# Elu of the first MoE handled in stages several products apart, with six tiles for the exponentials and another order of products

## The chip, the core and the metric

The program runs on one core of one Trainium2 chip. The metric is the device time of one execution in microseconds (us). Three timed runs of the kernel before gave 707.75, 708.32 and 710.72 us; the median is 708.32 us. The profiled execution took 708.1 us, 706.3 us of which are its span, from the first to the last instruction; 1.8 us lie around it.

## The reference

Attention with a pooled query gives `x` of 1152 tokens by 512; two feed-forward blocks follow. All is float32. The change concerns the first block:

```python
h = x @ w_in                                        # 1152x512 @ 512x2048
g = np.where(h > 0.0, h, alpha * (np.exp(np.minimum(h, 0.0)) - 1.0))   # Elu, alpha = 1
x = g @ w_out                                       # 1152x2048 @ 2048x512
```

The second block normalises `x` (root mean square), and computes `silu(xn @ w_gate) * (xn @ w_val) @ w_out`.

## The kernel before, in words

**Number format.** Every float32 operand is split in two parts, `h` (rounded) and `l` (the rest). A product with one 128-row slice is three matmuls, `h*h`, `l*h` and `h*l`, of 128 columns of weights against 384 tokens. Weights arrive as 64-bit words and are decoded on the chip. In the text a *matmul* is one of 128x384, a *product* is 12 of them (four slices, L216 to L218), a *half product* is 6, and a *group* (L712) is 6.

**Engines.** PE multiplies. ScalarE (ACT) does the Elu's Relu and Exp, the rounding to `h`, and two steps of each weight's decoding (L120, L122) and its rounding (L183). VectorE (DVE) does `max(exp - 1, v)`, called the *maximum* below (L237, L780), the sums of products, and three steps of the decoding (L131, L133, L136). GpSimd (POOL) computes the rest `l` (L64) and, for pairs of weights, the sums that the split product needs (L156 to L162). Each engine takes its instructions strictly in the order in which the program issues them: an instruction that waits holds up all behind it on its engine.

**The stream of weights.** `ws` is a generator of the decoding's steps. `ws.step(i, k)` issues the next k steps; the kernel calls it after every product, so that decoding is spread over the engines' queues. `ws.get(i)` issues steps until weight i is done. Weights are numbered w0 to w31 for the first block: per quarter q (four quarters of the 2048 hidden columns) four of `w_in` (8q to 8q+3), then four of `w_out` (8q+4 to 8q+7).

**The first block.** The tokens are three chunks c of 384, the hidden columns four quarters q of four slices i. `g(c, i)` is the Elu's output for a chunk and a slice.

- Quarter 0: twelve products, three of them (chunk 0, into the tile `fb`) at the end of attention, then nine in the order (i, c). Each is followed by `elu` (L230): Relu and Exp on ACT, the step before's rounding and rest (`flush`), the maximum on DVE.
- Quarters 1 to 3: for chunks 0 and 1 two slices at a time are computed as a 2x2 block product with seven multiplications (`Branch.m`, cases 1 to 7, one group each), chunk 2 with plain products (cases 8 and 9). Two branches, *even* and *odd*, make a quarter's *Elu stage* of 132 matmuls. Case 6 leaves a sum in the bank `b` that DVE reads for `u2` (L748), case 7 accumulates onto the same bank, after which DVE reads it for `u3` (L753), and case 4 accumulates once more. Results go through `Elu.out` (L769): the sum `v` (L774), Relu, Exp, then the maximum at the next `flush` and rounding and rest at the one after.
- After the stage come the quarter's *out products*: 12 products of `g` with `w_out` (`out1`, L841), for output slices m of 0 to 3 and chunks 2, 0, 1. Slice m=0 is done in halves: hidden slices 0 and 1 for all three chunks, then 2 and 3.
- `sums_from_x` (L798) makes the operands `ts` of the block product from `x`: four sums, four differences of 128x768 (L805, L809) on DVE, four roundings, four rests. It is stepped during quarter 0.
- In quarter 3 squares of `x` are added up for the root mean square (`Norm.square`, L668), and `Norm.sums` (L677) multiplies them by ones.

**Banks.** PSUM has eight banks. `bank()` (L645) hands out seven in turn; the eighth holds `wm` of the decoding, from the sixth bank on. A bank can be written again when its last reader is done.

Of the kernel before, what the change touches and what calls it, by code (L numbers as in the profile page):

```python
# [39 lines left out]
def tile_kernel(ctx: ExitStack, tc: tile.TileContext, qd, kd, vd, w1d, w2d, wgd, wvd, wod, rgd, outd):  # L40
# [207 lines left out]
    actx = ExitStack()  # L248
    ap = actx.enter_context(tc.tile_pool(name="attn", bufs=1))
    with tc.using_default_side("right"):  # L250
        sp = actx.enter_context(tc.tile_pool(name="psS", bufs=1, space=PSUM))
    pp = actx.enter_context(tc.tile_pool(name="psO", bufs=1, space=PSUM))
# [371 lines left out]
    early(2)  # L624
    for n in range(NE):
        elu(fb[:, n, 0:CH], ge[0][:, n, :], ge[1][:, n, :], lo_pool)
    actx.close()
# [8 lines left out]
    x2 = cp.tile([128, 4, NT], F32, name="x2")  # L636
    psb = [ctx.enter_context(tc.tile_pool(name="psB", bufs=5, space=PSUM))]
    nbank = 0

    def bank():  # L640

        nonlocal nbank
        n, nbank = nbank % 7, nbank + 1
        if n == 5 and len(psb) == 1:
            with tc.using_default_side("right"):  # L645
                psb.append(ctx.enter_context(tc.tile_pool(name="psC", bufs=2, space=PSUM)))
                ws.bank = ctx.enter_context(tc.tile_pool(name="psW", bufs=1, space=PSUM))
        return psb[n >= 5].tile([128, 512], F32, tag="b", name="b", bufs=2 if n >= 5 else 5)[:, 0:CH]
# [8 lines left out]
    th, tl = (tsp.tile([128, 12, CH], F32R, name=f"ts{a}", tag=f"ts{a}") for a in "hl")  # L657
    ts = [(xh[:, 0:2, cs(1)], xl[:, 0:2, cs(1)])] + [(th[:, 2 * n:2 * n + 2], tl[:, 2 * n:2 * n + 2]) for n in range(3)]
    sums_at = [[t.rearrange("p k c -> p (k c)")[:, a:a + 1024].rearrange("p (k c) -> p k c", k=8) for t in (th, tl)]
               for a in (2304, 3584)]  # L660

    class Norm:
# [40 lines left out]
    class Branch:  # L703
# [11 lines left out]
        def m(self, n):  # L715
# [10 lines left out]
            elif n == 2:  # L726
                self.group(self.a, a12, b21, False, True)
                flush()
                self.out(0, 0, self.a)
                self.both(n)  # L730
            elif n == 3:
                self.group(self.e, s(4), b22, False, True)
                flush()
                self.out(0, 1, self.e, self.u2)
            elif n == 4:
                self.group(self.b, a22, ts[3], False, True)
                flush()
                self.out(1, 0, self.b, self.m1)
            elif n == 5:
                self.e = bank()  # L740
                self.group(self.e, s(1), ts[0], True, False)
                flush()
            elif n == 6:
                self.b = bank()
                self.group(self.b, s(2), ts[1], True, False)
                flush()
                self.u2 = hp.tile([128, CH], F32, tag="e", name="u2", bufs=4)
                V.tensor_tensor(out=self.u2, in0=self.b, in1=self.m1, op=ALU.add)  # L748
            elif n == 7:
                self.group(self.b, s(3), ts[2], False, False)  # L750
                flush()
                self.u3 = self.pool.tile([128, CH], F32, tag="u3", name="u3", bufs=2)
                V.tensor_tensor(out=self.u3, in0=self.b, in1=self.m1, op=ALU.add)  # L753
                self.both(n)
            else:
                b = bank()
                product(b, w[n - 8], xchunk(2), True, True)
                flush()
                self.out(n - 8, 2, b)

    class Elu(Branch):
# [6 lines left out]

        def out(self, k, c, p, add=None):  # L769
            h, l = g_block(c, self.k + k)  # L770
# [5 lines left out]
            T.activation(out=e, in_=v, func=AF.Relu, scale=-1.0)  # L776
            T.activation(out=e, in_=e, func=AF.Exp, scale=-1.0)

            def second():
                V.scalar_tensor_tensor(out=e, in0=e, scalar=-1.0, in1=v, op0=ALU.add, op1=ALU.max)  # L780
                pending.append(third)

            def third():
                T.copy(h, e)  # L784
                lo_pool(l, e, h)

            pending.append(second)

        def both(self, n):
            if n == 7:  # L790
                self.out(1, 1, self.e, self.u3)
# [7 lines left out]
    def sums_from_x():  # L799

        r = x2.rearrange("p m c -> p (m c)")[:, NT:NT + 3072].rearrange("p (n k c) -> p n k c", n=4, k=2)
        b11, b12, b21, b22 = (r[:, n] for n in (0, 1, 2, 3))
        for n, (j, l) in enumerate(((0, 0), (0, 1), (1, 0), (1, 1))):
            h, l = (t[:, 2 * j:2 * j + 2, cs(l)] for t in (xh, xl))
            V.tensor_tensor(out=r[:, n], in0=f(h), in1=f(l), op=ALU.add)  # L805
            yield
        t1, t2, t3, t4 = b11, b22, b12, b21
        for n, o, a, b in ((0, t1, b12, b11), (2, t3, b22, b12), (1, t2, b22, t1), (3, t4, b21, t2)):
            V.tensor_tensor(out=o, in0=a, in1=b, op=ALU.subtract)  # L809
            yield  # L810
        for n, t in ((0, t1), (2, t3), (1, t2), (3, t4)):
            T.copy(ts[n][0], t)
            yield
            (lo_dve if n in (0, 3) else lo_pool)(ts[n][1], t, ts[n][0])
            yield

    sums_of_x = sums_from_x()

# [3 lines left out]
    for i in range(4):  # L822
        w = ws.get(i)
        for c in range(3):
            if c == 0 and i < NE:
                continue
            ps = bank()
            product(ps, w, xchunk(c), True, True)
            elu(ps, *g_block(c, i), lo_pool)
            if i > 1:  # L830
                next(sums_of_x)
        wi += 1

    for q in range(4):
        if q:
# [3 lines left out]
            run([(b, 1), (old, 4), (b, 8), (old, 3)], 2 * q + 2)  # L839
            run([(b, k) for k in (2, 9, 6, 5, 7, 4, 3)], 2 * q + 3)  # L840
            ws.limit = 2 * q + 4  # L841
            wi += 4

        def out1(c, m, b, then=None, ks=range(4)):
            product(b, ws.get(wi + m if q == 3 else wi), lambda k: g_block(c, k), True, True, ks)
            flush()
# [14 lines left out]
        if q < 3:  # L861
            for m in range(4):
                bs = [bank() for c in range(3)]
                for ks in ((0, 1), (2, 3)) if m == 0 else (range(4),):
                    for c in (2, 0, 1):
                        out1(c, m, bs[c], None, ks)
                        if q == m == 0:
                            next(sums_of_x, None)
                            next(sums_of_x, None)
                        ws.step(wi, 5 if len(ks) > 2 else 3)  # L870
                wi += 1
        else:
# [21 lines left out]
    class Gate(Branch):  # L894


        def __init__(self, n):
            super().__init__([ws.get(wi + 2 * n + k) for k in range(2)], up)
            self.sums, self.val, self.i = n + 6, n % 2, 2 * (n // 2)

        def out(self, k, c, p, add=None, into=None):
            d = u[c][:, self.i + k]
# [6 lines left out]
            else:  # L909
                pending.append(lambda: T.activation(out=d, in_=p, func=AF.Silu))  # L910

# [181 lines left out]
```

## Time and profile before

| | |
|---|---|
| median of three runs | 708.32 us (707.75 to 710.72) |
| profiled execution | 708.1 us, span 706.3 us |
| PE busy | 675.0 us, 96% |
| DVE, ACT, POOL busy | 509.3, 473.1, 451.4 us |
| attention and first products | 0 to 273 us |
| out products of quarter 0 | 273 to 306 us |
| quarters 1, 2, 3 | from 306 us to 482 us |
| second block | 482 to 706 us |

How to read it: the busy share of PE is an average. What a change is worth is read where PE stands idle: which instruction it waited for, how long, and at what clock it went on. The granted clock of a stretch is written as a share of full speed; it has two levels, 1.2 and 2.4 GHz, so 0.5 would be a stretch wholly at the lower one.

### The profile page before, as it was taken

The page shows a single profiled execution, that of the slowest core. Times are in us where ns is not written, and L with a number is a line of the kernel's source. Part 1 is how long each engine was busy: PE and PEld are TensorE (multiplying, and loading weights), DVE is VectorE, ACT ScalarE, POOL GpSimd, SP SyncE. Part 2 cuts the span into 40 slices and gives each one's busy share as a digit, 9 for nine tenths or more (in the row PEclk, how much of TensorE's full clock was granted, in tenths as well). Part 3 has the DMA queues.
Part 4 walks back from the last instruction along what each step waited for, and adds up shares of the span by engine and source line. Part 5 has one row for each costly group of instructions (what it writes and reads, how often), then busy time and mean ns, then how long its engine had stood idle before and what let it go on. Part 6 is the DMA issues. An engine that isn't in the chain of part 4 may idle for free. (4 is left out here: it accounts for less than half of the span.)

```text
span 706.3 us, 11416 instructions
## 1 busy us (share of the span) xinstructions
PE 675.0 (96%) x4149; PEld 663.4 (94%) x4149; DVE 509.3 (72%) x867; ACT 473.1 (67%) x924; POOL 451.4 (64%) x409
## 2 busy tenths in 40 slices
PE   8999999999999997997997898799999999999998
PEld 7999999999999996997996898799999999999997
DVE  7989989998998859855665664568778866867300
ACT  6888989888899868577547556654766655545400
POOL 5998889888895237676566474455898966233200
PEclk9999999999999999898999899899999999999999
DMA  5533332233221002230331132020234322303200
GB/s 167 178 110 127 101 115 84 93 131 130 98 86 47 1 31 90 90 120 30 105 106 60 60 112 67 31 90 31 70 111 141 104 85 90 120 1 120 97 34 33
DMA packets 21624, 61.75 MB, mean 87 GB/s; under 512 B 2752, under 2 KB 5056, under 8 KB 21568
## 3 DMA queue, kind: packets, MB, share of 16 engines
q1 hardware_dynamic: 21568, 61.03, 26.0%
q8 instruction: 32, 0.52, 0.3%
q14 instruction: 24, 0.20, 0.1%
HBM read 58.66 MB, written 2.36 MB: 86 GB/s over the span
## 5 line engine op out<-in xcount | busy, mean ns | idle before, releaser
L64 POOL TENSOR_TENSOR wl<-wt,wh 128x512 fp32r<-128x512 f32 x68 | 92.2, 1355 | 79.5 <-ACT wh L183 77.9
L70 DVE TENSOR_TENSOR ptl<-t,pth 128x384 fp32r<-128x384 f32 x216 | 106.7, 549 | 5.2 <-ACT pth L364 4.7
L342 DVE TENSOR_SCALAR_CACHE_REDUCE p<-s 128x1152 f32<-128x1152 f32 x72 | 97.3, 1353 | 14.7 <-PE s L338 14.0
L364 ACT CAST pth<-t 128x384 fp32r<-128x384 f32 x216 | 89.2, 488 | 21.6 <-PE t L356 20.8
L338 PE MATMUL s<-kd,qt 128*128 128x384 f32 x480 | 98.6, 342 | 1.8 <-DVE p L342 1.0
L347 ACT ACTIVATE p<-p,st 128x1152 f32<-128x1152 f32 x72 | 91.5, 1271 | 1.3 <-DVE p L342 1.1
L216 PE MATMUL b<-xh,wh 128*128 128x384 f32 x260 | 88.2, 339 | 0.0
L217 PE MATMUL b<-xl,wh 128*128 128x384 f32 x260 | 88.2, 339 | 0.0
L218 PE MATMUL b<-xh,wl 128*128 128x384 f32 x260 | 88.2, 339 | 0.0
L338 PEld LDWEIGHTS s<-kd,qt 128*128 128x128 f32 x480 | 81.2, 189 | 5.2 <-DVE p L342 2.7
L382 PE MATMUL o<-pth,vd 128*128 128x256 f32 (+1 forms) x288 | 84.4, 315 | 0.0
L356 PE MATMUL t<-ident,p 128*128 128x128 f32 x648 | 82.5, 273 | 0.0
L382 PE MATMUL o<-ptl,vd 128*128 128x256 f32 (+1 forms) x288 | 78.5, 295 | 0.0
L356 PEld LDWEIGHTS t<-ident,p 128*128 128x128 f32 x648 | 75.0, 141 | 2.0 <-ACT p L347 0.3
L120 ACT ACTIVATE we<-wr 128x512 uint32<-128x512 uint32 x68 | 45.5, 669 | 39.4 <-DMA wr<-in_w_dram 18.7
L122 ACT ACTIVATE wm<-wr 128x512 f32<-128x512 f32 x62 | 38.9, 628 | 30.4 <-DVE wt L136 30.2
L131 DVE TENSOR_SCALAR wm<-wm 128x512 f32<-128x512 f32 x62 | 43.0, 693 | 18.8 <-ACT wm L122 18.7
L216 PE MATMUL b<-gh,wh 128*128 128x384 f32 x144 | 50.3, 349 | 4.7 <-ACT gh L238 4.7
L382 PEld LDWEIGHTS o<-pth,vd 128*128 128x128 f32 x288 | 54.4, 189 | 0.3
L382 PEld LDWEIGHTS o<-ptl,vd 128*128 128x128 f32 x288 | 54.5, 189 | 0.0
L64 POOL TENSOR_TENSOR gl<-eg,gh 128x384 fp32r<-128x384 f32 x27 | 27.4, 1016 | 42.3 <-ACT gh L784 42.3
L217 PE MATMUL b<-gl,wh 128*128 128x384 f32 x144 | 50.1, 348 | 2.8 <-POOL gl L64 2.8
(200 smaller groups left out, 1808.3 us busy)
## 6 DMA issues: line engine op xcount, KB each, us to landing
wr<-in_w_dram SPq DMA_DIRECT2D x32, 512.0 KB, 3.2
rawq<-in_q_dram SPq DMA_DIRECT2D x15, 576.0 KB, 4.2
rawk<-in_k_dram SPq DMA_DIRECT2D x28, 288.0 KB, 2.9
wr<-in_wg_dram SPq DMA_DIRECT2D x12, 512.0 KB, 3.2
wr<-in_wv_dram SPq DMA_DIRECT2D x12, 512.0 KB, 3.2
wr<-in_wo_dram SPq DMA_DIRECT2D x12, 512.0 KB, 3.3
rawv<-in_v_dram SPq DMA_DIRECT2D x16, 288.0 KB, 2.8
out_dram<-o SPq DMA_DIRECT2D x12, 192.0 KB, 1.8
```

Of the source, the lines that this page charges most:

```text
L64: G.tensor_tensor(out=o, in0=i, in1=f(h), op=ALU.subtract)
L70: V.tensor_tensor(out=o, in0=i, in1=f(h), op=ALU.subtract)
L120: T.activation(out=e, in_=lo, func=AF.Copy, scale=0.93625 * 2.0 ** -29)
L216: PE.matmul(out, lhsT=wh[:, k, :], rhs=ah, start=first and k == 0, stop=False)
L217: PE.matmul(out, lhsT=wh[:, k, :], rhs=al, start=False, stop=False)
L218: PE.matmul(out, lhsT=wl[:, k, :], rhs=ah, start=False, stop=last and k == 3)
L338: PE.matmul(s[:, m, 0:384], lhsT=a, rhs=b[:, 384 * m:384 * m + 384], start=n == 0, stop=n == len(parts) - 1)
L342: V.tensor_scalar(out=pt, in0=s[:, :, 0:384], scalar1=-0.0625, scalar2=None, op0=ALU.mult, op1=ALU.min, accum_out=st[p][:, 0, TILES[i][4], :])
L347: T.activation(out=pt, in_=pt, func=AF.Exp, scale=-1.0, bias=st[p][:, 0, TILES[i][4], :], accum_out=st[p][:, 1, TILES[i][4], :])
L356: PE.transpose(ps[:, k, :], src[:, 128 * b:128 * b + 128], ident)
L364: T.copy(oh, re(ps))
L382: PE.matmul(self.o[:, 0:self.N], lhsT=v[:, b, :], rhs=(pth, ptl)[u][:, g["buf"], b, g["c0"]:320], start=self.n == 0, stop=self.n == 17)
```

## The change

In short: (1) `elu` and `Elu.out` become one function; each result's maximum is issued two calls of `flush` later, its rounding and rest three later, and `flush` is called within `elu`, after the sum. (2) The tiles `e` for the exponentials are six in place of three, in the block's own pool. (3) The sum `v` is written back into the product's bank (or into `u3`) in place of an own tile `v`. (4) In case 6, `u2` is issued ahead of `flush`. (5) The odd branch runs cases 6, 5, 2, 7, 9, 4, 3 in place of 2, 9, 6, 5, 7, 4, 3. (6) In quarters 0 to 2 the out products of m=0 and m=1 are both done in halves, so that six half products lie between the Elu stage and the first use of hidden slices 2 and 3; the weight of m=1 is needed three half products earlier. (7) `sums_from_x` issues its four sums before the first Elu, the differences one every three products, the rest between the out products. (8) The banks are four and three in place of five and two, and `wm` has its bank earlier. (9) The last addition of squares moves from POOL to DVE.

```diff
+    def defer(n, work):
+        pending.append([n, work])
     def flush():
-        now, pending[:] = list(pending), []
-        for work in now:
+        for item in pending:
+            item[0] -= 1
+        due = [work for n, work in pending if n == 0]
+        pending[:] = [item for item in pending if item[0]]
+        for work in due:
             work()
-    def elu(ps, gh, gl, lo):
-        e = hp.tile([128, CH], F32, tag="e", name="e", bufs=4)
-        T.activation(out=e, in_=ps, func=AF.Relu, scale=-1.0)
+    def elu(v, gh, gl, add=None, into=None):
+        e = gp.tile([128, CH], F32, tag="eg", name="eg", bufs=6)
+        if add is not None:
+            ps, v = v, v if into is None else into
+            V.tensor_tensor(out=v, in0=ps, in1=add, op=ALU.add)
+        flush()
+        T.activation(out=e, in_=v, func=AF.Relu, scale=-1.0)
         T.activation(out=e, in_=e, func=AF.Exp, scale=-1.0)
-        flush()
-        ws.step(wi, 1)
-        V.scalar_tensor_tensor(out=e, in0=e, scalar=-1.0, in1=ps, op0=ALU.add, op1=ALU.max)
-        pending.append(lambda: (T.copy(gh, e), lo(gl, e, gh)))
-        ws.step(wi, 2)
+        defer(2, lambda: V.scalar_tensor_tensor(out=e, in0=e, scalar=-1.0, in1=v, op0=ALU.add, op1=ALU.max))
+        defer(3, lambda: (T.copy(gh, e), lo_pool(gl, e, gh)))
...
+    for n in range(4):
+        next(sums_of_x)
+    for n in range(NE):
+        elu(fb[:, n, 0:CH], ge[0][:, n], ge[1][:, n])
+        ws.step(0, 3)
...
-                G.tensor_tensor(out=self.s, in0=self.s, in1=q, op=ALU.add)
+                (V if m == 3 else G).tensor_tensor(out=self.s, in0=self.s, in1=q, op=ALU.add)
...
             elif n == 6:
                 self.b = bank()
                 self.group(self.b, s(2), ts[1], True, False)
-                flush()
                 self.u2 = hp.tile([128, CH], F32, tag="e", name="u2", bufs=4)
                 V.tensor_tensor(out=self.u2, in0=self.b, in1=self.m1, op=ALU.add)
+                flush()
...
-            v = p
-            if add is not None:
-                v = gp.tile([128, CH], F32, tag="v", name="v", bufs=3)
-                V.tensor_tensor(out=v, in0=p, in1=add, op=ALU.add)
-            e = gp.tile([128, CH], F32, tag="eg", name="eg", bufs=3)
...
+        def out(self, k, c, p, add=None, into=None):
+            elu(p, *g_block(c, self.k + k), add, into)
...
-            if i > 1:
+            if i > 1 and c == 2:
                 next(sums_of_x)
...
-            run([(b, k) for k in (2, 9, 6, 5, 7, 4, 3)], 2 * q + 3)
+            run([(b, k) for k in (6, 5, 2, 7, 9, 4, 3)], 2 * q + 3)
...
-            for m in range(4):
-                bs = [bank() for c in range(3)]
-                for ks in ((0, 1), (2, 3)) if m == 0 else (range(4),):
-                    for c in (2, 0, 1):
-                        out1(c, m, bs[c], None, ks)
...
+            for m, ks in ((0, (0, 1)), (1, (0, 1)), (0, (2, 3)), (1, (2, 3)), (2, range(4)), (3, range(4))):
+                for c in (2, 0, 1):
...
+                    out1(c, m, banks[m, c], None, ks)
```

What stands in the queue of VectorE around the end of quarter 0's nine products: `L237` (after: `L245`) is the maximum, `L805` and `L809` (after: `L658`) are the sums and differences of `sums_from_x`, `L131` to `L136` the decoding. Before:

```order
L805 TENSOR_TENSOR x_3532<-xh,xl 128x768
L237 SCALAR_TENSOR_TENSOR e<-e,b 128x384
L131 TENSOR_SCALAR wm<-wm 128x512
L805 TENSOR_TENSOR x_3532<-xh,xl 128x768
L133 SCALAR_TENSOR_TENSOR wm<-wm,we 128x512
L237 SCALAR_TENSOR_TENSOR e<-e,b 128x384
L136 SCALAR_TENSOR_TENSOR wt<-wr,wm 128x512
L805 TENSOR_TENSOR x_3532<-xh,xl 128x768
L237 SCALAR_TENSOR_TENSOR e<-e,b 128x384
L809 TENSOR_TENSOR x_3532<-x_3532 128x768 x3
L131 TENSOR_SCALAR wm<-wm 128x512
```

The last `L237` is the maximum of the ninth product. Now:

```order
L133 SCALAR_TENSOR_TENSOR wm<-wm,we 128x512
L136 SCALAR_TENSOR_TENSOR wt<-wr,wm 128x512
L245 SCALAR_TENSOR_TENSOR eg<-eg,b 128x384
L658 TENSOR_TENSOR x_3508<-x_3508 128x768
L245 SCALAR_TENSOR_TENSOR eg<-eg,b 128x384
L658 TENSOR_TENSOR x_3508<-x_3508 128x768
L131 TENSOR_SCALAR wm<-wm 128x512
L245 SCALAR_TENSOR_TENSOR eg<-eg,b 128x384
L658 TENSOR_TENSOR x_3508<-x_3508 128x768
L133 SCALAR_TENSOR_TENSOR wm<-wm,we 128x512
```

The third `L245` is the ninth product's. In place of sums, differences lie between the last maxima; the four sums stand ahead of the first maximum of the block.

What stands in VectorE's queue in quarter 1's odd branch around `u2` (`L748`, after: `L778`) and `u3` (`L753`, after: `L784`); `L774` (after: `L241`) is the sum `v`, `L780` (after: `L245`) the maximum. Before:

```order
L780 SCALAR_TENSOR_TENSOR eg<-eg,b 128x384
L774 TENSOR_TENSOR v<-b,u_4059 128x384
L136 SCALAR_TENSOR_TENSOR wt<-wr,wm 128x512
L780 SCALAR_TENSOR_TENSOR eg<-eg,v 128x384
L780 SCALAR_TENSOR_TENSOR eg<-eg,b 128x384 x2
L748 TENSOR_TENSOR u_4253<-b,m_4149 128x384
L753 TENSOR_TENSOR u_4274<-b,m_4149 128x384
L774 TENSOR_TENSOR v<-b,u_4274 128x384
```

Now:

```order
L245 SCALAR_TENSOR_TENSOR eg<-eg,b 128x384
L241 TENSOR_TENSOR b<-b,u_4056 128x384
L245 SCALAR_TENSOR_TENSOR eg<-eg,b 128x384
L778 TENSOR_TENSOR u_4204<-b,m_4141 128x384
L245 SCALAR_TENSOR_TENSOR eg<-eg,b 128x384
L131 TENSOR_SCALAR wm<-wm 128x512
L245 SCALAR_TENSOR_TENSOR eg<-eg,b 128x384
L133 SCALAR_TENSOR_TENSOR wm<-wm,we 128x512
L136 SCALAR_TENSOR_TENSOR wt<-wr,wm 128x512
L784 TENSOR_TENSOR u_4241<-b,m_4141 128x384
L241 TENSOR_TENSOR u_4241<-b,u_4241 128x384
```

Before, three maxima stood between the sum `v` and `u2`; now one does, and it belongs to a result two calls older. Between `u2` and `u3` there now stand two maxima and a weight's three steps. `v` has become an in-place sum in `b`.

## Rows read from the trace of the kernel before

**Rows 1.** The page: busy time and share by engine; a step of decoding, mean ns.

```profile
PE 675.0 (96%) x4149; PEld 663.4 (94%) x4149; DVE 509.3 (72%) x867; ACT 473.1 (67%) x924; POOL 451.4 (64%) x409
...
L131 DVE TENSOR_SCALAR wm<-wm 128x512 f32<-128x512 f32 x62 | 43.0, 693 | 18.8 <-ACT wm L122 18.7
```

**Rows 2.** Whom PE waited for: us in total, times, longest.

```profile
PE b L712 <- DVE u L748: 12.8, 3, 4.7
PE b L216 <- ACT gh L238: 4.7, 1, 4.7
PE b L217 <- POOL gl L64: 2.8, 3, 1.4
PE b L680 <- POOL sq L675: 2.4, 2, 1.2
PE b L712 <- DVE u L753: 1.9, 3, 0.7
```

**Rows 3.** Windows: length, engines' busy time (instructions), PE's clock, DMA share, GB/s.

```profile
276.60:286.40 9.80, 4.31 (x13) 3.80 (x13) 9.73 (x11) 5.58 (x10) 8.74 (x6) 0.65 0.16 54
325.80:337.60 11.80, 7.42 (x26) 7.02 (x26) 7.16 (x13) 8.21 (x18) 6.26 (x6) 0.71 0.13 44
381.70:392.20 10.50, 5.55 (x16) 5.05 (x17) 5.68 (x10) 5.21 (x12) 4.86 (x5) 0.67 0.16 50
439.70:450.20 10.50, 5.21 (x15) 4.70 (x16) 5.58 (x11) 6.33 (x14) 5.23 (x5) 0.68 0.08 32
550.00:600.00 50.00, 50.00 (x287) 50.00 (x286) 35.28 (x61) 28.28 (x49) 36.83 (x33) 1.00 0.28 95
```

**Rows 4.** Timeline of VectorE at the first gap: start, duration, instruction.

```profile
275.83 1.95 DVE L805 TENSOR_TENSOR x<-xh,xl 128x768 f32<-128x768 f32 x1
...
278.30 0.54 DVE L237 SCALAR_TENSOR_TENSOR e<-e,b 128x384 f32<-128x384 f32 x1
...
279.36 0.94 DVE L805 TENSOR_TENSOR x<-xh,xl 128x768 f32<-128x768 f32 x1
280.23 0.54 DVE L237 SCALAR_TENSOR_TENSOR e<-e,b 128x384 f32<-128x384 f32 x1
```

**Rows 5.** Timeline at the first gap, PE and GpSimd: start, duration, instruction, idle before.

```profile
279.46 1.70 POOL L64 TENSOR_TENSOR gl<-e,gh 128x384 fp32r<-128x384 f32 x1 [0.83 <-ACT gh L238]
...
281.37 0.69 PE L216 MATMUL b<-gh,wh 128*128 128x384 f32 x1 [4.66 <-ACT gh L238]
...
282.80 2.00 POOL L64 TENSOR_TENSOR wl<-wt,wh 128x512 fp32r<-128x512 f32 x1
...
282.89 0.69 PE L217 MATMUL b<-gl,wh 128*128 128x384 f32 x1 [0.83 <-POOL gl L64]
```

**Rows 6.** Timeline of VectorE at the second gap.

```profile
325.81 0.56 DVE L780 SCALAR_TENSOR_TENSOR eg<-eg,v 128x384 f32<-128x384 f32 x1 [0.67 <-ACT eg L777]
327.16 0.55 DVE L780 SCALAR_TENSOR_TENSOR eg<-eg,b 128x384 f32<-128x384 f32 x1 [0.80 <-ACT eg L777]
328.51 0.55 DVE L780 SCALAR_TENSOR_TENSOR eg<-eg,b 128x384 f32<-128x384 f32 x1 [0.79 <-ACT eg L777]
328.98 0.55 DVE L748 TENSOR_TENSOR u<-b,m 128x384 f32<-128x384 f32 x1
330.96 0.56 DVE L753 TENSOR_TENSOR u<-b,m 128x384 f32<-128x384 f32 x1 [1.43 <-PE b L712]
```

**Rows 7.** Timeline of ScalarE at the second gap.

```profile
326.02 0.48 ACT L776 ACTIVATE eg<-b 128x384 f32<-128x384 f32 x1
...
327.37 0.48 ACT L776 ACTIVATE eg<-b 128x384 f32<-128x384 f32 x1
...
328.31 0.64 ACT L120 ACTIVATE we<-wr 128x512 uint32<-128x512 uint32 x1
```

**Rows 8.** Start of quarter 1: a pair's sums on GpSimd, and PE's first use.

```profile
304.17 2.40 POOL L64 TENSOR_TENSOR tsl<-sf,tsh 128x1024 fp32r<-128x1024 f32 x1
...
307.21 0.33 PE L712 MATMUL b<-tsh,tsl 128*128 128x384 f32 x1
```

More of the change, by code (lines that the diff above doesn't have):

```diff
@@ L249, in tile_kernel @@
     ap = actx.enter_context(tc.tile_pool(name="attn", bufs=1))
+    sctx = ExitStack()
     with tc.using_default_side("right"):
-        sp = actx.enter_context(tc.tile_pool(name="psS", bufs=1, space=PSUM))
+        sp = sctx.enter_context(tc.tile_pool(name="psS", bufs=1, space=PSUM))
     pp = actx.enter_context(tc.tile_pool(name="psO", bufs=1, space=PSUM))
@@ L636, in tile_kernel, with sums_from_x @@
     x2 = cp.tile([128, 4, NT], F32, name="x2")
-    psb = [ctx.enter_context(tc.tile_pool(name="psB", bufs=5, space=PSUM))]
+    th, tl = (tsp.tile([128, 12, CH], F32R, name=f"ts{a}", tag=f"ts{a}") for a in "hl")
+    ts = [(xh[:, 0:2, cs(1)], xl[:, 0:2, cs(1)])] + [(th[:, 2 * n:2 * n + 2], tl[:, 2 * n:2 * n + 2]) for n in range(3)]
+    sums_at = [[t.rearrange("p k c -> p (k c)")[:, a:a + 1024].rearrange("p (k c) -> p k c", k=8) for t in (th, tl)]
+               for a in (2304, 3584)]
+    def sums_from_x():
+        r = x2.rearrange("p m c -> p (m c)")[:, NT:NT + 3072].rearrange("p (n k c) -> p n k c", n=4, k=2)
+        b11, b12, b21, b22 = (r[:, n] for n in (0, 1, 3, 2))
+        for b, j, l in ((b11, 0, 0), (b21, 1, 0), (b12, 0, 1), (b22, 1, 1)):
+            h, x = (f(t[:, 2 * j:2 * j + 2, cs(l)]) for t in (xh, xl))
+            V.tensor_tensor(out=b, in0=h, in1=x, op=ALU.add)
+            yield
+        t1, t2, t3, t4 = b11, b22, b12, b21
+        for n, o, a, b in ((0, t1, b12, b11), (2, t3, b22, b12), (1, t2, b22, t1), (3, t4, b21, t2)):
+            V.tensor_tensor(out=o, in0=a, in1=b, op=ALU.subtract)
+            yield
+        for n, t in ((0, t1), (2, t3), (1, t2), (3, t4)):
+            T.copy(ts[n][0], t)
+            yield
+            (lo_dve if n in (0, 3) else lo_pool)(ts[n][1], t, ts[n][0])
+            yield
+    sums_of_x = sums_from_x()
+    for n in range(4):
[3 more added lines that the diff above has]
+        ws.step(0, 3)
+    sctx.close()
+    psb = [ctx.enter_context(tc.tile_pool(name="psB", bufs=4, space=PSUM))]
+    ws.bank = ctx.enter_context(tc.tile_pool(name="psW", bufs=1, space=PSUM))
     nbank = 0
@@ L643, in bank @@
         n, nbank = nbank % 7, nbank + 1
-        if n == 5 and len(psb) == 1:
+        if n == 4 and len(psb) == 1:
             with tc.using_default_side("right"):
-                psb.append(ctx.enter_context(tc.tile_pool(name="psC", bufs=2, space=PSUM)))
-                ws.bank = ctx.enter_context(tc.tile_pool(name="psW", bufs=1, space=PSUM))
-        return psb[n >= 5].tile([128, 512], F32, tag="b", name="b", bufs=2 if n >= 5 else 5)[:, 0:CH]
+                psb.append(ctx.enter_context(tc.tile_pool(name="psC", bufs=3, space=PSUM)))
+        return psb[n >= 4].tile([128, 512], F32, tag="b", name="b", bufs=3 if n >= 4 else 4)[:, 0:CH]
     g_at = [gp.tile([128, 12 - NE, CH], F32R, name=f"g{n}", tag=f"g{n}") for n in "hl"]
@@ L655, in g_block @@
         return [t[:, n] for t in ge] if n < NE else [t[:, n - NE] for t in g_at]
[L657 to L660, printed above, removed]
     class Norm:
@@ L767, in __init__, with flush @@
             self.sums = n
-        def out(self, k, c, p, add=None):
-            h, l = g_block(c, self.k + k)
-            v = p
-            if add is not None:
-                v = gp.tile([128, CH], F32, tag="v", name="v", bufs=3)
-                V.tensor_tensor(out=v, in0=p, in1=add, op=ALU.add)
-            e = gp.tile([128, CH], F32, tag="eg", name="eg", bufs=3)
[L776 to L787, printed above, removed]
+        def flush(self):
+            pass
+        def out(self, k, c, p, add=None, into=None):
+            elu(p, *g_block(c, self.k + k), add, into)
         def both(self, n):
             if n == 7:
-                self.out(1, 1, self.e, self.u3)
+                self.out(1, 1, self.e, self.u3, self.u3)
     def run(order, limit, k=1):
@@ L797, in run @@
             ws.step(wi, 3 * k if m > 7 else k)
[L799 to L817, printed above, removed]
     ws.pools.append((mp, WB - NE))
@@ L828, in tile_kernel @@
             product(ps, w, xchunk(c), True, True)
-            elu(ps, *g_block(c, i), lo_pool)
-            if i > 1:
+            elu(ps, *g_block(c, i))
+            ws.step(wi, 3)
+            if i > 1 and c == 2:
                 next(sums_of_x)
@@ L844, in out1 @@
         def out1(c, m, b, then=None, ks=range(4)):
-            product(b, ws.get(wi + m if q == 3 else wi), lambda k: g_block(c, k), True, True, ks)
+            product(b, ws.get(8 * q + 4 + m), lambda k: g_block(c, k), True, True, ks)
             flush()
@@ L861, in tile_kernel @@
         if q < 3:
-            for m in range(4):
-                bs = [bank() for c in range(3)]
-                for ks in ((0, 1), (2, 3)) if m == 0 else (range(4),):
-                    for c in (2, 0, 1):
-                        out1(c, m, bs[c], None, ks)
-                        if q == m == 0:
+            banks = {}
+            for m, ks in ((0, (0, 1)), (1, (0, 1)), (0, (2, 3)), (1, (2, 3)), (2, range(4)), (3, range(4))):
+                for c in (2, 0, 1):
+                    if (m, c) not in banks:
+                        banks[m, c] = bank()
+                    out1(c, m, banks[m, c], None, ks)
+                    if q == 0 and (m, ks[0]) != (1, 2):
+                        next(sums_of_x, None)
+                        if m == 1:
                             next(sums_of_x, None)
-                            next(sums_of_x, None)
-                        ws.step(wi, 5 if len(ks) > 2 else 3)
-                wi += 1
+                    ws.step(wi, 5 if len(ks) > 2 else 3 if ks[0] == 0 else 2)
+                if ks[-1] == 3:
+                    wi += 1
         else:
@@ L909, in out @@
             else:
-                pending.append(lambda: T.activation(out=d, in_=p, func=AF.Silu))
+                defer(1, lambda: T.activation(out=d, in_=p, func=AF.Silu))
         def both(self, n):
```

14 lines of the change are left out of this document (7 added, 7 removed).

## The prediction

> **What bounds the kernel now.** I read the page's busy times first: PE is busy for 675.0 of 706.3 us [rows 1], so time can only be won where PE stands idle or runs slowly. The list of PE's waits comes next [rows 2]: three waits for `u2` (`L748`) make 12.8 us, one for the rounding of quarter 0's last Elu result (`L238`) 4.7, three for its rests `gl` 2.8, two for the sums of squares 2.4, three for `u3` (`L753`) 1.9. Then one window for each of the four long gaps [rows 3]: the reader is to see that PE is idle for part of it and that its clock, 0.65 to 0.71 in the mean, lies between the two levels, so that matmuls after the gap run slowly too.
>
> The price of a gap, clock included, is the window less what its matmuls take at full speed. Full speed is 50 us for 287 matmuls, one of which only reaches in from the edge: 0.1745 us each [rows 3]. With the one that reaches in left out of each gap's count: 9.80 - 12 x 0.1745 = 7.7; 11.80 - 25 x 0.1745 = 7.4; 10.50 - 15 x 0.1745 = 7.9; 10.50 - 14 x 0.1745 = 8.1. Together 31.1 us. Idle are 20.1 of these (lengths less PE's busy time), so 11.0, or 2.75 a gap, is lower clock. Outside them lie the two other waits for `gl`, 2.8 - 0.83 = 2.0 us [rows 2, 5], and the 2.4 us for squares.
>
> **Gap 1, end of quarter 0.** PE stops at 281.37 - 4.66 = 276.7 [rows 5], after 18 matmuls of half products and three more; the ninth product had thus ended 21 x 0.1745 = 3.7 us earlier, at 273.0, called T. Its Elu result could be used at T + 8.4 (rounded, 281.37) and T + 9.9 (rest, 282.89). PE needed it at T + 3.7. After the change 36 + 3 matmuls come first: T + 6.8, and the rest 0.2 later. That alone takes 3.1 us off. The latency falls as well: two sums of 1.95 and 0.94 us stand on DVE ahead of the last two maxima [rows 4]. These sums go to a place ahead of the block's first maximum, where four of them, by the same two durations 4 to 8 us, delay the maxima by that much with eight products of 2.1 us still to come. Between the last maxima there are now differences in their place, same shape, 1 to 2 us each. From the start of the nine products, T - 9 x 2.09 = 254.2, DVE's new queue holds, up to the ninth maximum, four sums of 0.94 (POOL has nothing to do then), twelve maxima of 0.54, three differences of 1.95 and eleven decoding steps of 0.69 [rows 1, 4]: 3.8 + 6.5 + 5.9 + 7.6 = 23.8 us, to 278.0 or T + 5, if it needn't wait (before: 280.23 + 0.54, T + 7.8). The rounding follows 0.5 later, at T + 5.5; the rest ends at about T + 8, since POOL first takes a weight's rest (up to 2.0) and the eighth result's (up to 1.7) [rows 5]. PE would wait about 1 us. Bounds: nothing, or, if the latency stayed as it is, 9.9 - 7.0 = 2.9 and the clock's 2.75. I take 2.0, near the walk, since the queues are full there. The other weight needed earlier (that of m=1, at T + 3.1) has its rounding ahead of the eighth result's Relu in ACT's queue; were it late, its delay would add to this gap.
>
> **Gaps 2 to 4, the odd branch.** In [rows 6] `u2` stands behind three maxima that each wait 0.67 to 0.80 us for ACT's Exp; their distance of 1.35 us is ACT's Relu, Exp and rounding of one result [rows 7]. PE has only case 5 (1.05 us) to do before case 7 needs the bank that `u2` reads. Afterwards `u2` is behind one maximum, whose Exp is two results older, and PE has cases 5 and 2 to do. In time from the stage's start, with 1.05 us a group: case 6 ends at 15.7, `u2` runs to 16.5, case 7 begins at 17.8. That wait goes, with 1.3 us in hand. What is late next is `u3`: case 7 ends at 18.8, case 4 begins after case 9 at 20.9. Ahead of `u3` in DVE's queue are two maxima and the three decoding steps of 0.69 us [rows 1], and the second maximum needs ACT. ACT has 12 results x 1.35 = 16.2 us and about nine decoding steps of 0.6 [rows 7], 21.6 us, plus copies and a pair's rounding, in a stage of 132 x 0.1745 = 23.0 us: it is full. If it is 1.6 us behind when it comes to the result of case 3 (sum ready at 15.4), its Exp ends at 15.4 + 1.6 + 1.0 = 18.0, the maximum at 18.6, two decoding steps at 20.0, and `u3` at 20.6, just in time.
>
> The change adds a wait here. A sum kept in its bank holds the bank until its maximum, and case 5 takes the bank in which the even branch's case 4 left its sum. That maximum stands on DVE behind the sum of case 3, which PE finishes at 14.7: 14.8 + 0.56 + 0.55 = 15.9, against case 5's start at 15.7. So 0.2 us a stage; behind the waiting matmul stands everything on PE, and `u2` has been read by then. Each stage costs between 0.2 us and, if ACT is 3 us further behind than I think, 3 + 2.75. I take 1.0 each, 3.0 in all. The six tiles for `e` cost nothing: they only drop a wait for POOL's reading. In-place sums are the same count of instructions as before.
>
> **The rest.** In quarters 1 and 2 the last result gets eight half products of 1.05 us in place of five before it is used; the wait for `gl` there goes (1.4, the longest). In quarter 3 the order of halves is unchanged and the rounding is issued one call later, behind two decoding steps of 0.6: 0.6 becomes about 1.2. Gain 0.8, bounds 2.0 and -2. The last addition of squares needs 0.55 on DVE (the two-input row of [rows 6]) where POOL took about 1.0 (2.4 us of waits end with it): 0.5 less of each wait, 1.0 in all; bounds: nothing, and 2.4 + 2 x 2.75 = 7.9 if the waits went whole and the clock with them stayed up. The issue order of weights' DMAs is unchanged; each still goes out after a decoding step on DVE, so it follows DVE's queue. Banks of four and three, and an earlier `wm`, remove nothing from PE's path: 0.
>
> In [rows 4, 5] one 768-wide sum took 1.95 us and the next 0.94, and the `gl` that began 0.1 us after the short one took 1.70. The Trainium skill, SBUF — State Buffer, section Who interferes with whom, says that a VectorE instruction with two SBUF inputs contends with a GpSimd one that reads SBUF, and that whichever begins first holds the other up. By that rule, with which these rows agree, the moved addition of squares can itself be blocked, by up to 1.0 us (1.95 - 0.94), and the 1.0 gained would become a loss of 1.0: 2 us on the total.
>
> Sum: 31.1 - 2.0 - 3.0 + 0.8 + 1.0 = 27.9 us off the span of 706.3: 678.4. With the 1.8 us around it 680.2; the median lies 0.2 above the profiled execution, 708.32 to 708.1. Forecast 680.
>
> **Rivals.**
> (a) ACT becomes the bound of the Elu stages. For it: 21.6 us and more in 23.0. Against: it was held by DVE's sums before and now takes Relu and Exp ahead of the older results' rounding, and nothing but `u3` and the copy of case 1 is wanted of it in time. If each stage loses 3.2 us of waiting at case 4 and 2.75 of clock, 18 come back, 3 of which are counted: 695.
> (b) The stream of weights becomes the bound. For it: the sums of the first pair were ready at 304.17 + 2.40 = 306.57 and used at 307.21 [rows 8], 0.64 us to spare, and PE now comes 5.7 us earlier (7.7 - 2.0). If the stream does not move, PE waits 5.1 us and loses 2.75 more: 688. Against: the decoding stood in the same DVE queue as the sums and differences, most of which now go earlier.
> (c) `u2` is late as before, held by the one maximum before it because ACT is far behind: the gaps 2 to 4 (23.4) stay, 701. Against: that result is three calls old.
> (d) Slower: the banks. Seven banks go round while each result holds one until its maximum two calls later. If maxima run 4 to 5 us behind, case 5 and case 9 of each odd branch both wait, and each such wait costs what the present gaps do, 7.7: 6 x 7.7 = 46 in place of the 27.9 won, 726. It decides from the point where case 5 and case 9 wait some 2 us more than I count in each stage and the clock falls there. Against: 0.2 us at case 5 by the count above, and none at case 9. The Trainium skill, Perfetto Trace Analysis, section Optimization Strategy, has the same gap repeating on the engine that should be full as a sign that there is not enough SBUF or PSUM for the next tile; the trace's own repeating gap [rows 6] is an ordering on DVE instead, and no run here yet shows banks as the cause.
>
> **How the numbers follow.** The forecast's case has 0.68, (a) 0.13, (b) 0.11, (c) 0.04, (d) 0.03, and 0.01 stays for no change. What a measurement can tell from no change here is about 0.5%, 3.5 us. All cases but (d) and the last are faster by more: 0.96, 0.01, 0.03. The forecast's own range is 671 (no wait left in gaps 1 to 4 but 0.2 a stage, and part of the squares' clock won: 37 off) to 688 (5.6 in gap 1, 2.5 a stage). Towards (a) and (b) I extend it to 696; what is left out are (c), (d) and the tails, under 2 in 10.
>
> **What would show it.** PE's waits for `u2` gone from the list; no window in quarters 0 to 2 with a clock below 0.9; a short wait for a `gl` some 7 us after the ninth product; in each odd branch a wait of a few tenths at case 5 that DVE's maximum ends. Wrong would be: a wait of over 2 us at case 4 on `u3` with ACT ending the waits ahead of it (a); a wait at the first use of a pair's sums in quarter 1 that POOL ends (b); waits of several microseconds on maxima ahead of a bank's first matmul (d); or a gap 1 that is as long as before.

## The result, and the profile after

The changed kernel takes 688.93 us (median of 4 runs, 687.01 to 689.21), the kernel before 708.47 beside it: a ratio of 0.9713 [0.9685, 0.9741]. The forecast was 680, the range 671 to 696. Faster, as forecast, and inside the range, but of the 28 us expected 19 came. The profiled execution has a span of 687.3 us, 19.0 below the one before.

Where TensorE waits in the changed kernel, 250 to 480 us, answers to [rows 2]. The columns are: who waits, for whom, us in total, times, longest.

```profile
PE b L216 <- ACT wh L183: 5.3, 2, 3.5
PE b L218 <- POOL wl L64: 2.8, 2, 2.1
PE b L217 <- POOL gl L64: 2.0, 1, 2.0
PE b L711 <- DVE sq L706: 0.7, 1, 0.7
PE b L721 <- DVE rr L715: 0.4, 1, 0.4
```

The waits for `u2` and `u3` of the Elu stages are gone, and of those for Elu results one is left. New are four waits for a weight, `wh` (its rounding) and `wl` (its rest), 8.1 us together. Windows answer to [rows 3]: gap 1, where gaps 2 and 3 were, and two places where no long gap was before.

```profile
276.00:290.00 14.00, 12.01 (x60) 11.69 (x59) 11.12 (x15) 10.87 (x22) 13.46 (x9) 0.88 0.28 94
420.00:440.00 20.00, 14.43 (x69) 13.73 (x68) 10.36 (x18) 12.65 (x26) 9.03 (x10) 0.83 0.16 54
470.00:480.00 10.00, 7.46 (x33) 6.72 (x32) 6.35 (x11) 5.88 (x12) 4.26 (x4) 0.83 0.15 52
320.00:340.00 20.00, 19.89 (x114) 19.49 (x113) 15.26 (x27) 15.22 (x31) 13.49 (x13) 1.00 0.28 95
365.00:375.00 10.00, 9.93 (x57) 9.61 (x56) 6.54 (x13) 9.16 (x20) 6.88 (x8) 1.00 0.15 53
```

Priced as in the prediction, length less (matmuls - 1) x 0.1745: gap 1 costs 14 - 59 x 0.1745 = 3.7 us. The window at the first of the old `u2` gaps has 0.3, that at the second 0.2, and from 410 to 420, at the third, it is 0.2 as well: 0.7. Between 420 and 440, at the start of quarter 3's out products, 20 - 68 x 0.1745 = 8.1 us are lost. So 31.1 - 3.7 - 0.7 - 8.1 = 18.6 of the 19.0. The remaining 0.4 is the rest of the program, where the second block's late weight (470 to 480: 4.4) eats what shorter waits for `gl` and for squares give. The 8.1 and 4.4 are not all new: counted over the same matmuls, the first 72 of quarter 3's out products lost 2.5 us before and 8.2 now, the 171 after them 2.9 and 4.3.

The new gap on TensorE: start, duration, instruction, idle before and who ended it.

```profile
426.02 0.33 PE L218 MATMUL b<-geh,wl 128*128 128x384 f32 x1
429.87 0.44 PE L216 MATMUL b<-geh,wh 128*128 128x384 f32 x1 [3.52 <-ACT wh L183]
...
432.61 0.69 PE L218 MATMUL b<-geh,wl 128*128 128x384 f32 x1 [2.06 <-POOL wl L64]
433.10 0.52 PE L216 MATMUL b<-geh,wh 128*128 128x384 f32 x1
...
437.20 0.34 PE L217 MATMUL b<-gl,wh 128*128 128x384 f32 x1
```

Three half products of six matmuls run (423.04 to 426.2), then the fourth, which needs weight 31, waits. Matmuls of 0.52 us afterwards are those at the lower clock (the granted clock is 0.50 from 433.0 to 436.5). ScalarE's queue shows why that weight is late:

```profile
421.25 0.61 ACT L183 CAST wh<-wt 128x512 fp32r<-128x512 f32 x1
...
425.89 1.28 ACT L874 ACT_TABLE_LOAD   x1
...
427.29 0.49 ACT L246 CAST gh<-eg 128x384 fp32r<-128x384 f32 x1
427.69 0.66 ACT L120 ACTIVATE we<-wr 128x512 uint32<-128x512 uint32 x1
428.25 0.61 ACT L122 ACTIVATE wm<-wr 128x512 f32<-128x512 f32 x1
428.80 0.49 ACT L246 CAST gh<-eg 128x384 fp32r<-128x384 f32 x1
429.20 0.61 ACT L183 CAST wh<-wt 128x512 fp32r<-128x512 f32 x1
```

The cast at 421.25 is weight 30's, the one at 429.20 weight 31's: between them stand the last Elu results, the table load for the square root, and the next weight's decoding. In the kernel before, weight 31 was cast ahead of them; there the two instructions lie ten microseconds apart in the other order:

```profile
443.62 0.60 ACT L183 CAST wh<-wt 128x512 fp32r<-128x512 f32 x1
...
453.65 1.28 ACT L873 ACT_TABLE_LOAD   x1
```

The reason is in the change, in a number that the prediction passed over. Each out product of quarters 0 to 2 ends with some steps of the weight stream (`ws.step`). Before, a quarter's loop issued 6 x 3 + 9 x 5 = 63; the new loop, with `5 if len(ks) > 2 else 3 if ks[0] == 0 else 2`, issues 6 x 3 + 6 x 2 + 6 x 5 = 60. A weight is nine steps (two on ScalarE, three of decoding, three of splitting, one between); three quarters make nine. When quarter 3's out products begin, exactly one weight less has been issued. The traces agree: by TensorE's first matmul of these products, ScalarE has started 32 casts of weights (`L183`) in the kernel before (at 450.81) and 31 in the changed one (at 423.04).

### The profile page after: what moved, and what is told of

Read it like the earlier page. It is cut to its first block, busy times and chain, and to the rows that moved or that the text cites. A ratio compares the mean times of both kernels' runs of the same rounds, so it can differ in the third digit from the quotient of the medians.

```text
span 687.3 us, 11390 instructions
## 1 busy us (share of the span) xinstructions
PE 667.6 (97%) x4149; PEld 657.1 (96%) x4149; DVE 502.9 (73%) x870; ACT 471.3 (69%) x924; POOL 447.2 (65%) x406
## 4 chain that ended last, share of the span: by engine, by line
PE 80%; ACT 6%; POOL 5%; DVE 5%; issue 1%; DMA 0%; DVEq 0%; ACTq 0%; SPq 0%; POOLq 0%
PE b L743 15%; PE s L346 12%; PE o L390 11%; PE b L218 10%; PE b L217 10%; PE b L216 10%; PE t L364 10%; POOL gl L64 2%; POOL wl L64 2%; ACT eg L243 1%; ACT xh L728 1%; ACT eg L244 1%; DVE x L940 1%; ACT wh L183 1%; DVE wt L136 1%
## 5 line engine op out<-in xcount | busy, mean ns | idle before, releaser
L131 DVE TENSOR_SCALAR wm<-wm 128x512 f32<-128x512 f32 x63 | 43.7, 693 | 21.1 <-ACT wm L122 21.1
L64 POOL TENSOR_TENSOR gl<-eg,gh 128x384 fp32r<-128x384 f32 x36 | 39.1, 1103 | 18.8 <-ACT gh L246 18.7
L216 PEld LDWEIGHTS b<-xh,wh 128*128 128x128 f32 x260 | 49.2, 189 | 2.1 <-ACT wh L183 2.1
```

The source lines that it names most:

```text
L64: G.tensor_tensor(out=o, in0=i, in1=f(h), op=ALU.subtract)
L216: PE.matmul(out, lhsT=wh[:, k, :], rhs=ah, start=first and k == 0, stop=False)
```

## The experiments

My theory after the result: the stream is short of steps, not of time. Rivals: the stream is as fast as its DMAs and engines allow and had lived on the old gap 4; or the table load holds the weight. The order of the products of the Elu stages, the deferral and the tiles were tested after it.

**e1, more steps.**

```diff
-    ws.step(wi, 5 if len(ks) > 2 else 3 if ks[0] == 0 else 2)
+    ws.step(wi, 5 if len(ks) > 2 else 3)
```

> The changed kernel, with 3 steps of the weight stream in place of 2 after each second half product of quarters 0 to 2: 66 steps a quarter, where the kernel before had 63 and the changed one has 60. Theory (too few steps): the changed kernel is 9 steps, about one weight, behind when quarter 3's out products begin, so weight 31's rounding stands on ScalarE behind the last Elu results and the table load. With 66 steps it is issued before them: the wait at 429.87 (7.96 us with its clock) goes, and the late weight at 472.99 (about 3 us more than before) too: 678 us, 676 to 681. Rival (rate): the stream is as fast as its DMAs and engines allow, and only the old gap 4 gave it time; then the wait stays or comes back at another weight, and the time is 686 to 690. Rival (table): the table load holds the rounding, the wait shrinks by 1.5 at most.

678.5 us, 0.9575 [0.9554, 0.9596]: the theory's number, and both rivals fall. TensorE's waits in 250 to 520 us:

```profile
PE b L217 <- POOL gl L64: 3.9, 2, 2.0
PE b L216 <- ACT u L931: 1.1, 1, 1.1
PE b L743 <- DVE u L784: 0.5, 1, 0.5
```

No wait for a weight is left, and the mean clock is 1.00. Behind the weight a wait of 1.92 us for the last rest `gl` comes to light in quarter 3, which the late weight had hidden. Two windows, at that place and at the second block's late weight:

```profile
420.00:430.00 10.00, 7.88 (x44) 7.31 (x43) 5.61 (x10) 7.58 (x16) 6.53 (x6) 1.00 0.16 55
...
460.00:470.00 10.00, 8.75 (x50) 8.19 (x50) 8.46 (x13) 7.61 (x14) 5.42 (x4) 1.00 0.16 52
```

They cost 2.5 and 1.4 us in place of 8.1 and 4.4: 8.6 won, where I had expected 11. Another 1.6 are gap 1, which costs 2.1 here (last section). The spans of the two profiled executions, 687.3 and 675.8 us, differ by 11.5, so some 1.3 lie elsewhere. The total thus hit the mark with some luck.

**e2, the kernel before with fewer steps.** The same edit the other way, in the kernel before: `5 if len(ks) > 2 else 3 if ks[0] == 0 else 2`.

> The kernel before, with nothing changed but the steps of the weight stream: 2 in place of 3 after each second half product of quarters 0 to 2, so 60 a quarter as in the changed kernel. Theory (too few steps): weight 31's rounding moves on ScalarE from 443.6 us to behind the table load at 454, its rest to about 458, where TensorE wants it at about 455: a wait of 2 to 3 us and 2.75 of clock, and a late weight in the second block: 714 us, 711 to 718. Rival (rate): the stages of this kernel leave the stream all the time it needs, 708.5, within 1.5.

713.29 us, 1.0063 [1.0038, 1.0087]. Here the time is lost although all four long gaps are still there to give the stream time. On ScalarE and TensorE:

```profile
453.19 1.28 ACT L873 ACT_TABLE_LOAD   x1
...
456.50 0.61 ACT L183 CAST wh<-wt 128x512 fp32r<-128x512 f32 x1
```

```profile
457.17 0.44 PE L216 MATMUL b<-geh,wh 128*128 128x384 f32 x1 [2.78 <-ACT wh L183]
458.95 0.69 PE L218 MATMUL b<-geh,wl 128*128 128x384 f32 x1 [1.16 <-POOL wl L64]
```

The cast has moved behind the table load, as expected, and the wait is there. The stream's count of steps is shown as the cause from both sides.

**e3, the table load later.** The line with `AF.Sqrt` moves behind the first chunk of quarter 3.

> The changed kernel, with ScalarE's dummy Sqrt, and so its table load of 1.28 us, issued behind quarter 3's first chunk in place of ahead of it. Theory (too few steps): weight 31's rounding comes 1.5 us earlier and no more, TensorE waits 5.6 - 1.5 = 4.1 us, the clock's loss stays: 687.5, 686 to 689. Rival (table): what holds the weight is the table load; then most of the 8 us of this gap goes, 681 to 683. If the load lands in the normalisation's chain instead, slower, up to 692.

685.73 us, 0.9679 [0.9662, 0.9695]: 3 us of the 8, just below the theory's range and far from the rival's. In the profiled execution, the slowest of its four, the span is 1.3 shorter: the wait for `wh` at this place fell from 3.52 to 1.99, the wait for `wl` stayed (2.13). What the medians show beyond that goes with TensorE's mean clock, which is on record for every execution. Here it is 0.990 in the profiled one (span 686.0 us) and 0.992 to 0.993 in the others (683.7 to 684.0); in the changed kernel it is 0.989 to 0.990 in three (687.0 to 687.4) and 0.992 in one (685.2). At equal clock, 0.990 or 0.992, the move wins 1.0 and 1.2 us, about the theory's 1.5.

**e7, the old order of out products.** Quarters 0 to 2 with the loop of the kernel before, and so with its 63 steps.

> The changed kernel with the old order of out products in quarters 0 to 2 (only the first output block in halves, its second halves after three half products), and with that the old 63 steps a quarter. Theory (too few steps): gap 1 is back, about 1.99 + 3.1 us idle and 2.75 of clock = 7.9 in place of 3.7, the short waits for gl in quarters 1 and 2 cost 1 more, but weight 31 is in time again (-8.0, and -3 in the second block): 683, 680 to 686, that is faster than the changed kernel although a part of it is undone. Rival (rate): only the losses come, 693 to 696.

688.02 us, 0.9705 [0.9691, 0.972], the same as the changed kernel, and between the ranges of the theory and the rival. Its windows:

```profile
270.00:290.00 20.00, 15.46 (x70) 14.57 (x69) 15.66 (x19) 13.78 (x28) 16.43 (x12) 0.83 0.16 53
330.00:340.00 10.00, 8.30 (x46) 7.42 (x45) 7.26 (x14) 7.20 (x15) 8.23 (x8) 1.00 0.33 107
380.00:390.00 10.00, 8.10 (x42) 6.88 (x41) 7.64 (x15) 7.88 (x17) 7.47 (x7) 1.00 0.24 88
430.00:440.00 10.00, 7.95 (x45) 7.38 (x44) 7.06 (x12) 8.79 (x18) 6.27 (x6) 1.00 0.16 55
```

Gap 1 costs 20 - 69 x 0.1745 = 8.0, as expected. But the windows of quarters 1 and 2, with waits for `gh` and `gl` of the last results, cost 2.1 and 2.8 us, where I had 1 for both, and quarter 3 keeps 2.3, the wait that e1 laid bare. So the new order is worth 4.3 in quarter 0 and some 4 to 5 in the two others: its steps had cost about as much as it won.

The experiments that follow, g3 apart, stand on e1's kernel, since its gaps are not mixed with the late weight.

**f1, f2, f3: the order on VectorE and the deferral.** f1 undoes the odd branch's order and puts the flush ahead of `u2` again, f2 undoes the deferral, f3 both:

```diff
-    run([(b, k) for k in (6, 5, 2, 7, 9, 4, 3)], 2 * q + 3)      # f1, f3; flush() ahead of u2 too
+    run([(b, k) for k in (2, 9, 6, 5, 7, 4, 3)], 2 * q + 3)
-    defer(2, lambda: V...);  defer(3, lambda: (T.copy...         # f2, f3
+    defer(1, lambda: V...);  defer(2, lambda: (T.copy...
```

> The kernel with 66 stream steps (678.5 us), with the odd branch as it was: order (2, 9, 6, 5, 7, 4, 3), and the flush of maxima ahead of u2 in case 6; the deferral by two and three products stays. On VectorE u2 stands behind four maxima and a decoding step again, but each maximum is one result older. Theory (order on VectorE): u2 is late again, the Exps one result of 1.35 us earlier than in the kernel before, so some 4.3 - 1.35 = 2.9 us of wait and 2.75 of clock in each of three stages: +17, 695 us, 686 to 699. Rival (deferral): older Exps suffice and the order is not needed: 679 to 681.

> The kernel with 66 stream steps, with maxima one product after their result and roundings two after, in place of two and three; the new order of the odd branch and u2 ahead of the flush stay. Theory (order on VectorE): u2 has nothing young ahead of it, its waits stay away; the last maxima ahead of u3 wait for ScalarE, a few tenths in each stage; gap 1's results come earlier by up to 1 us: 678.5, 676 to 681. Rival (deferral): it is what took the waits of the Elu stages away, 690 or more.

> Both undone together on the kernel with 66 stream steps: old order, flush ahead of u2, maxima one and roundings two products after. Both theories: the three waits of 4.3 us for u2 with 2.75 of clock each are back, 678.5 + 21 = 700, 695 to 702, and what stays won is gap 1 (4 us) and squares. If it stays under 690, what removed the waits was neither, but the sums kept in their banks or the six tiles.

| odd branch \ deferral | two and three | one and two |
|---|---|---|
| new order, `u2` first | 678.5 (e1) | 678.0 (f2) |
| old order, flush first | 681.19 (f1) | 696.24 (f3) |

Ratios to before: 0.962 [0.9598, 0.9642] for f1, 0.9573 [0.9553, 0.9593] for f2, 0.9818 [0.9783, 0.9853] for f3. My expectation of 695 for f1 was wrong. Undone alone, the order costs 2.7 us and the deferral nothing; undone together they cost 18 us. The waits of f3, 250 to 450 us, and then of f1, 300 to 450:

```profile
PE b L743 <- DVE u L779: 10.2, 3, 3.9
PE b L217 <- POOL gl L64: 2.2, 1, 2.2
```

```profile
PE b L743 <- DVE u L784: 2.6, 3, 1.2
PE b L217 <- POOL gl L64: 1.9, 1, 1.9
PE b L743 <- DVE u L779: 0.9, 2, 0.7
```

With older maxima ahead of it, `u2` comes in time even in the old place; I had credited the deferral with one result of 1.35 us, and it took 9.3 of the 10.2 us of waiting for `u2`, while the waits for `u3` (`L784`) are 2.6 us in f1 and 1.9 in f3.

**g3, the order alone on the kernel before.** The same two edits, nothing else.

> The kernel before with two edits alone: the odd branch in order (6, 5, 2, 7, 9, 4, 3), and u2 ahead of the flush in case 6. Everything else is the old kernel, with 63 stream steps. Theory (order on VectorE is enough by itself): the three waits for u2 go with the clock's loss, 23.4 less 0.5 to 1 each for what is late next: 687, 685 to 691. Rival (needs the deferral or the banks too): maxima and sums hold u3 instead, 693 to 705.

704.05 us, 0.9925 [0.9905, 0.9946]: 5 us in place of the 22 expected. Waits from 250 to 480 us:

```profile
PE b L217 <- POOL gl L64: 5.9, 8, 1.1
PE b L216 <- ACT gh L238: 4.7, 1, 4.7
PE b L216 <- ACT gh L784: 3.9, 2, 3.3
PE b L712 <- DVE u L747: 3.8, 2, 2.0
PE b L712 <- DVE u L753: 1.4, 2, 0.9
```

The waits for `u2` fall from 12.8 to 3.8 us, but TensorE now arrives earlier at the out products and waits there for the roundings (`L784`) and rests of the last results. So "the order on VectorE is enough by itself" is wrong as I had put it: it moves the gap, and other parts of the change have to cover its new place. That the new out order is one of them e7 suggests, where waits for `gh` and `gl` come back at this place with the old one; whether the rest lies in the banks or tiles was not tried on this kernel.

**f4, the youngest result last.** In quarter 0 the second half products take chunks 0, 1, 2 in place of 2, 0, 1.

> The kernel with 66 stream steps, and in quarter 0 the second half products in order of chunks 0, 1, 2 in place of 2, 0, 1: the product that needs the last Elu result comes 2.1 us later. Theory (the wait at 282.25 is for the youngest result's rest alone): its 1.99 us go, 676.3, 675 to 677.5. Rival (queue of GpSimd): the two results before it are late too, and the wait only moves to another chunk: 677.5 to 679.

676.58 us, 0.9546 [0.9528, 0.9564]. The wait at the end of quarter 0 is gone whole (TensorE is busy throughout 270 to 290 us), as the theory had it.

**h1, three tiles.** f2 with `bufs=3` for the exponentials.

> The kernel with 66 steps and the old deferral (one and two products, 678.0 us), with three tiles for exponentials in place of six. As predicted for the change the tiles cost and bring nothing on TensorE's path, a ScalarE wait for GpSimd's reading apart: 678 to 680. Rival (tiles): with three, a Relu waits until GpSimd has read the result three back, maxima and u2 or u3 behind it come late as in the kernel before with the new order alone (704.0), 685 to 700.

682.44 us, 0.9634 [0.9606, 0.9663], 4.4 above f2: between the two expectations. The Elu stages don't mind (waits for `u2` 1.6 us, in f2 1.5). Gap 1 does:

```profile
281.63 0.44 PE L216 MATMUL b<-gh,wh 128*128 128x384 f32 x1 [0.91 <-ACT gh L246]
284.68 0.44 PE L217 MATMUL b<-gl,wh 128*128 128x384 f32 x1 [2.61 <-POOL gl L64]
```

In f2 the one wait here is 2.18 us. By windows from 276 to 292 us the stretch costs 5.9 against 2.2: 1.3 of the difference is longer waiting, the rest is the clock, 0.89 against 1.00 in the mean. From 250 to 300 us ScalarE's Relu (`L243`) waits 2.3 us for GpSimd's rests `gl` and `gel`, in f2 not at all, which is what the rival names. The executions with a mean clock of 0.997 have spans of 680.1 to 680.8 us in h1 and 677.9 in f2. So the six tiles bring something, in quarter 0.

**g2, squares back on GpSimd**, on f4's kernel.

> The kernel with 66 steps and chunks in order 0, 1, 2 (676.6 us), with the last addition of squares back on GpSimd. As predicted for the change, an addition takes 1.0 us there and 0.55 on VectorE: 0.5 more in each of two waits, 677.6; if the clock falls after them as in the kernel before, up to 681. Rival (one engine stands in the other's way): no difference, 676 to 677, or faster.

675.25 us, 0.9525 [0.9508, 0.9541], no worse than f4: the moved addition brings nothing. TensorE waits 0.6 us for `sq` here and 0.3 in f4, but f4 waits longer elsewhere (1.1 against 0.3 for `u` at `L931`, 0.5 against none for `rr`).

**g1, a better quarter 3?** On f4's kernel, with e3's move, and the eight steps of the first halves behind the second ones.

> The kernel with 66 steps and chunks in order 0, 1, 2 (676.6 us), in quarter 3 with the table load behind the first chunk and the eight stream steps of the first four half products moved behind the second ones. In the kernel with 66 steps the last rest gl of quarter 3 ends at 428.6: its rounding waits 1.28 us for the table load, and one weight's rest of 1.29 stands ahead of it on GpSimd. Theory (these two hold it): the wait of 1.9 us goes, 674.5, 673.5 to 676. Rival (the product itself is late): at most 0.5 of it goes, 676 to 677.

676.22 us, 0.9539 [0.9525, 0.9553], no better than f4. The wait for `gl` goes, but TensorE now waits further on, in the normalisation (400 to 520 us; f4 has 0.3 and 0.5 for these two):

```profile
PE b L711 <- DVE sq L706: 1.7, 2, 1.4
PE b L721 <- DVE rr L715: 1.6, 2, 1.5
```

The table load does not explain these: it begins at 433.44, after the wait of 1.4 has ended (433.05), and the wait of 1.5 ends at 447.32. What holds the normalisation was not tested.

The version that beats both kernels is thus f4, with or without g2's edit: 675 to 677 us. f4, g1 and g2 can't be told apart by their intervals. The 12 us below the changed kernel are two small edits, one count of steps and one order of chunks.

## Why the prediction was right, and where it failed

- **Gap 1: 2.0 forecast, 3.7 measured.** The wait itself came out at 1.99 us for `gl`, but that is luck: the walk had given about 1, and 2.0 was picked near it because the queues are full there. I had left the clock's share out of the value and only in the bound, and the sign "no window in quarters 0 to 2 with a clock below 0.9" failed here (0.88). The walk was wrong, too. VectorE was ahead of my count: the last maximum ends at 277.24, 3.6 us after the ninth product (273.68, the wait's start less 40 x 0.1745), not 5. What is late is GpSimd, which has been busy without a break since 273.56:

```profile
273.56 4.41 POOL L64 TENSOR_TENSOR gl<-eg,gh 128x384 fp32r<-128x384 f32 x3
277.92 2.03 POOL L64 TENSOR_TENSOR wl<-wt,wh 128x512 fp32r<-128x512 f32 x1
279.90 2.70 POOL L64 TENSOR_TENSOR gl<-eg,gh 128x384 fp32r<-128x384 f32 x2
```

  The same rest takes 1.01 us elsewhere (427.86 in the same trace); here two take 2.70, while VectorE has a two-input subtraction at 280.03 that itself takes 1.70, against 0.95 for one of the same shape at 283.77:

```profile
280.03 1.70 DVE L70 TENSOR_TENSOR xl<-x,xh 128x768 fp32r<-128x768 f32 x1
...
283.77 0.95 DVE L70 TENSOR_TENSOR tsl<-x,tsh 128x768 fp32r<-128x768 f32 x1
```

  The Trainium skill, SBUF — State Buffer, section Who interferes with whom, has such pairs hold each other up; these rows agree. I had allowed for the weight's rest, not for three results' rests ahead of it.
- **Gaps 2 to 4: 3.0 forecast, 0.7 measured.** The mechanism held: `u2` gone, `u3` just in time, rivals (a), (c) and (d) did not come. Of the few tenths that I had named at case 5 nothing shows in the list of waits, and these windows leave no room for more than 0.3. What I had not seen is that the change removes this wait twice over (f1, f2), and that the old order with the old deferral would have kept it (f3).
- **Six tiles: "cost nothing".** True of the Elu stages; in gap 1 they are worth 3.7 us between the profiled executions of h1 and f2, of which 1.3 is waiting and the rest clock.
- **Quarter 3, the step that failed.** "In quarter 3 the order of halves is unchanged" is true, and I priced only the Elu rounding there. The weights of these halves were taken as given. Rival (b) had the right mechanism, a late weight, but at another place (quarter 1's first pair of sums, where nothing waits) and for another reason: "if the stream does not move", while the change itself moved it, by 63 to 60 steps. And the wait for the last `gl`, put at 1.2, lay hidden behind it with 1.92 (e1).
- **Squares: 1.0 forecast, nothing (g2).** The additions took what I had counted, 0.56 us on VectorE and 1.0 on GpSimd, and none of the three was held up, so the loss of 1.0 that the prediction weighed did not come either. With quarters 1 to 3 expected at +0.8, all outside the four gaps should have given 1.8; it lost 8.1 in quarter 3 and won 0.4.

Sum: 27.9 - 1.7 (gap 1) + 2.3 (gaps 2 to 4) - 8.1 (quarter 3) - 1.4 (the rest, 0.4 for 1.8) = 19.0, the difference of the spans. The forecast's own range ended at 688; 688.93 lies in the part that I had added for the rivals (a) and (b), and neither came as I had described it.

## What to carry to other kernels

Where a side stream (weights, prefetches) is advanced by counted steps between pieces of main work, count the steps before and after any rewrite of those loops: three fewer in each of three loops made one weight late, giving them back (and three more) took 10 us off, and the profile showed it only as a late operand far from the edit. A long wait can be overdetermined: two edits may each remove it, and an edit that works in one kernel moves the gap in another, so undo parts singly and together. And when a gap closes, look for what it had covered: the next late thing stands right behind it.

## What the runs showed of the hardware

Two gaps alike did not cost the same. In the changed kernel and in e1, TensorE waits 1.99 us at the same matmul of quarter 0, after tens of microseconds without a break. In the first the granted clock is 0.88 over 276 to 290 us, and the stretch costs 3.7; in e1 it is 1.00:

```profile
276.00:290.00 14.00, 12.01 (x69) 11.69 (x68) 12.68 (x18) 11.04 (x21) 14.00 (x10) 1.00 0.33 114
```

That is 14 - 68 x 0.1745 = 2.1 us, the wait and nothing else. The change from one kernel to the other need not be the reason: the four executions of e1, one and the same kernel, have mean clocks of 1.000, 0.997, 1.000 and 0.995 and spans of 675.8, 677.4, 676.0 and 679.0 us. The clock falls in some executions and not in others, and where it fell in the two that were not profiled is not on record. What decides between the two levels here the runs do not show; a gap of this length can be priced only from both sides.
